# An attention and GLU block on one core: LN2 per tile, GLU in halves, VectorE's exp tiles moved ahead, new scheduler durations

## Chip, core and metric

One core of one Trainium2 chip. The metric is the device time of one execution in microseconds; medians are of several executions. The TensorE clock is given as the granted share of full speed.

## The reference, cut

```python
h  = x + attention(layernorm(x))          # S = 2048, D = 640, 32 heads of 20
h2 = h + (gelu(ln(h) @ w_gate) * (ln(h) @ w_up)) @ w_down   # Df = 1728
```

All tensors are bf16. Terms used below: *QK* is the matmul of queries with keys that makes the scores, *exp* the exponential of the softmax, *PV* the matmul of these exponentials with the values; LN2 is the layernorm before the GLU, whose matmuls are gate, up and down; an *eviction* copies a result out of PSUM. The softmax takes 32 x 2048 x 2048 = 134 million exponentials, and these decide how the kernel is built.

## The kernel before

The kernel describes its work as operations with dependencies and an assumed duration each. While it is built, a list scheduler of its own runs them on paper and fixes each engine's order. Engines then run in that order, each waiting for semaphores.

Attention goes through seven chunks of queries (512, 512, 256, 256, 256, 128, 128). A *tile* is 512 columns of scores of one head. ScalarE gets *units* of three and two tiles in turn, PSUM banks 0 to 2 and 3 to 4; VectorE gets 250 of the 2048 tiles and computes their exponential with integer tricks. Work of the chunk before (output projection `wo`, LN2, GLU) is background of a lower priority.

The heads have 20 channels, so a QK matmul uses 32 of TensorE's 128 rows. Head `j` of a group of four takes row group `j`:

```python
tiles += [(s_, g, kb, j) for g in gs for kb in range(NT // nk) for j in range(4)]
# ...
def qk_mms(out, x, kk):                       # ... cut
    return lambda eng: eng.matmul(out()[:, kk * nq:(kk + 1) * nq],
        kt_all[32 * j:32 * j + 32, g, kt * 128:(kt + 1) * 128],
        qt_all[32 * j:32 * j + 32, q0 // 512, g, q0 % 512:q0 % 512 + nq],
        start=True, stop=True, tile_position=(32 * j, 0), skip_group_check=True)
# ... in unit(u): QK of the unit, then QK of VectorE's tile, if the unit has one
qk = op("pe", fns, 0.215, P_QK, mode="row", ...)
xd = dtile[u]
if xd:
    qd = op("pe", [qk_mms(lambda: bank(bd), xd, kk) for kk in ...], 0.08,
            P_QK + 0.5, mode="row", ..., after=[qk])
```

When TensorE was little used in the last 3.4 us of the scheduler's time, the scheduler puts filler matmuls (`pad`: four small ones side by side; `warm`: one large one) into its free time, and pads beside a PV too. They are meant to keep its clock up.

Of the kernel before, what the change touches and what calls it, by code (L numbers as in the profile page):

```python
# [17 lines left out]
WARM_WIN, WARM_MIN = 3.4, 0.5  # L18
PAD_WIN, PAD_MIN = 3.4, 0.42
PE_AGE = 1.5  # L20

MODE_SWITCH = {"pe": 0.105, "act": 1.28}
# [19 lines left out]
class Sched:  # L42
# [43 lines left out]
    def schedule(self):  # L86
# [22 lines left out]
        while done < total:  # L109
# [4 lines left out]
            for e in ENGINES:  # L114
# [70 lines left out]
                if e == "pe" and self.pad is not None and o.tag and o.tag[0] == "O":  # L185
                    while recent and recent[0][0] < t - PAD_WIN:
                        recent.popleft()
                    u = sum(x for _, x in recent) + o.util
                    while u < PAD_MIN * PAD_WIN and o.util < 1.1:
                        o.fns = o.fns + self.pad  # L190
                        o.dur += 0.215
                        o.util += 0.213
                        u += 0.213
                    live = o.i not in self.final
# [111 lines left out]
PV_QUADS = 2  # L306
D_LAG = 8
PR, PR2 = 12, 6
ND = 4
D_PER_SLOT = (8,) * len(SIZES)  # L310
D_SLOT0 = 2
D_FIRST, D_SPAN = 1, 16
# [5 lines left out]
def bass_sequential_preLN__mha_block__glu_gated_geglu__prompt_kernel(  # L318
# [12 lines left out]
    with ExitStack() as es:  # L331
# [10 lines left out]
        def c_mm(n, passes=1):  # L342
            return 0.001 + passes * n / 2400.0
# [174 lines left out]
        def ln_rsqrt(t0, n, prio, table=False, sqrt=False):  # L518

            y = rs[:, t0:t0 + n]  # L520
            a, b = nw[:, 0, 0:n], nw[:, 1, 0:n]
            ts = range(t0, t0 + n)
            k16, ks = ("mv16", t0), ("sd16", t0)
            rk = [("rs", t) for t in ts]
            v = lambda fn, r, w: op("dve", fn, 0.17, prio, reads=r, writes=w)
            d = v if table or sqrt else lambda fn, r, w: op(POOL, fn, 0.25, prio, reads=r, writes=w)
            d(I("tensor_copy", mv16[:, t0:t0 + n, :], mv[:, t0:t0 + n, :]), [("mv", t) for t in ts], [k16])
            d(I("tensor_scalar", sd16[:, t0:t0 + n], mv16[:, t0:t0 + n, 1], LN_EPS, None, ALU.add), [k16], [ks])
            d(I("tensor_copy", mu[:, t0:t0 + n], mv16[:, t0:t0 + n, 0]), [k16], [("mu", t) for t in ts])
            if sqrt:  # L530
                op("act", I("activation", sd16[:, t0:t0 + n], sd16[:, t0:t0 + n], ACT.Sqrt), 0.2, 1, reads=[ks], writes=[ks])
                v(I("reciprocal", y, sd16[:, t0:t0 + n]), [ks], rk)
                return
            if table:
                op("act", I("activation", sd16[:, t0:t0 + n], sd16[:, t0:t0 + n], ACT.Sqrt), 0.2, -1, mode="sqrt", reads=[ks],
                   writes=[ks])
                v(I("reciprocal", y, sd16[:, t0:t0 + n]), [ks], rk)
                return
            d(I("tensor_copy", a, sd16[:, t0:t0 + n]), [ks], ["nw0"])
            d(I("tensor_scalar", y.bitcast(I32), a.bitcast(I32), -0.5, RSQRT_MAGIC, ALU.mult, ALU.add), ["nw0"], rk)  # L540
            for _ in range(2):
                d(I("tensor_tensor", b, y, y, ALU.mult), rk, ["nw1"])
                d(I("tensor_tensor", b, b, a, ALU.mult), ["nw0", "nw1"], ["nw1"])
                d(I("tensor_scalar", b, b, -0.5, 1.5, ALU.mult, ALU.add), ["nw1"], ["nw1"])
                d(I("tensor_tensor", y, y, b, ALU.mult), ["nw1"] + rk, rk)
            d(I("tensor_tensor", sd16[:, t0:t0 + n], a, y, ALU.mult), ["nw0"] + rk, [ks])
            v(I("reciprocal", y, sd16[:, t0:t0 + n]), [ks], rk)
# [219 lines left out]
        units, ubank, dtile, ends = [], [], [], []  # L767
        i, in_slot = 0, {}
        while i < len(tiles):
# [9 lines left out]
            if k[1] < want and tiles[i][0] == s_:  # L779
                dtile.append(tiles[i])  # L780
                k[1] += 1
                i += 1
            else:
                dtile.append(None)
            k[0] += 1
            ends.append(i)
        assert all(k[1] % 2 == 0 for k in in_slot.values())
        d_tiles = set(x for x in dtile if x)
# [42 lines left out]
        def unit(u):  # L831
# [52 lines left out]
            while pv_wait:  # L884
# [17 lines left out]
                if len(quads) < PV_QUADS and not final:  # L902
                    pv_wait[0:0] = [x for h in quads for x in h]
                    return

                for have in quads:
                    for x in list(d_done):
                        if u - x_unit[x[2]] >= D_LAG and x[2][3] not in [y[2][3] for y in have]:
                            have.append(x)
                            d_done.remove(x)  # L910
                while final and d_done:
                    have = []
                    for x in list(d_done):
                        if x[2][3] not in [y[2][3] for y in have]:
# [20 lines left out]
                if final:  # L935
                    sc.final.add(pv)
                    assert not d_done and not d_raw
# [3 lines left out]
        def base(c):  # L941
            n = CHUNKS[c][1]
            if n == 128:
                return 2 + (c == len(CHUNKS) - 1)
            return 2 * (c % 2) if n < 512 else 0

        def epilogue(s_, bk):
# [13 lines left out]
            for tt in range(4):  # L961
                op("pe", lambda eng, tt=tt: eng.transpose(bank(b2)[:, tt * 128:(tt + 1) * 128],
                                                          osb[:, s, tt * 128:(tt + 1) * 128], identf[:]),
                   c_mm(128, 4), P_EPI, mode="full", reads=[("osb", s), "identf"], writes=[key], acq=[b2] if tt == 0 else [],
# [21 lines left out]
        def post(c, banks, tail):  # L986
# [27 lines left out]
            ln_rsqrt(q0 // 128, nt, p, table=tail)  # L1014
            if tail:
                op("act", I("activation", nm[:, 1:2], off0[:, 0:1], ACT.Gelu_apprx_tanh), 0.2, -1, mode="gelu",
                   reads=["off0"], writes=["warmge"], after=(sc.lw[("sd16", q0 // 128)],))
            for tt in range(tb, tb + nt):
                t = q0 // 128 + tt - tb
                ln_apply("dve", h_sb[:, tt, :], xn_t[:, t % 2, :], ("xn", t % 2), t, [("h", tt, 0), ("h", tt, 1)], p)  # L1020
# [7 lines left out]
            hk = [("hnT", tt) for tt in range(tb, tb + nt)]  # L1028
            hdone = []
            fn_ = 512 // nq  # L1030
            nb = -(-NF // fn_)

            def mms(k, w, wkey, after):
                bk, key = Bank(*banks), ("bk", sc_id())
                for fi in range(min(fn_, NF - k * fn_)):
                    f = k * fn_ + fi
                    for a in range(NA):
                        st = fi == 0 and a == 0
                        op("pe", lambda eng, a=a, f=f, fi=fi: eng.matmul(  # L1039
                            bank(bk)[:, fi * nq:(fi + 1) * nq], w[:, a, F0[f]:F0[f] + 128], hnT[:, a, 128 * tb:128 * tb + nq],  # L1040
                            start=(a == 0), stop=(a == NA - 1)),
                           c_mm(nq), p, mode="full", util=nq / 2400.0, reads=hk + [wkey], writes=[key], acq=[bk] if st else [],
                           after=after if st else ())
                return bk, key

            def cols(k):
                return min(512, (NF - k * fn_) * nq)

            def hv(k, w):
                return ha_f[:, hb + 512 * k:hb + 512 * k + w]  # L1050

            def hkeys(k):
                return [("ha", u) for u in range((hb + 512 * k) // 256, (hb + 512 * k + cols(k)) // 256)]

            if tail:
                for k in range(nb):
                    i = k % 2
                    bg, kg = mms(k, wg, "wg", hdone[k - 2:k - 1] if k >= 2 else ())
                    w = cols(k)
                    s16, fv = zb[:, i, 0:w], hv(k, w)  # L1060
                    op("act", lambda eng, bg=bg, s16=s16, w=w: eng.activation(s16, bank(bg, w), ACT.Gelu_apprx_tanh),
                       c_act(w), -1, mode="gelu", reads=[kg], writes=[("zb", i)], rel=[bg])
                    bu, ku = mms(k, wu, "wu", ())
                    hdone.append(op("dve", lambda eng, bu=bu, s16=s16, fv=fv, w=w: eng.tensor_tensor(  # L1064
                        fv, s16, bank(bu, w), ALU.mult), c_dve(w), p, reads=[ku, ("zb", i)], writes=hkeys(k),
                        rel=[bu]))
            else:

                cp, gl = [], []
                for k in range(nb):  # L1070
                    bg, kg = mms(k, wg, "wg", tuple(x for key in hkeys(k) for x in sc.rd.get(key, ())))
                    w = cols(k)
                    fv = hv(k, w)
                    cp.append(op("dve", lambda eng, bg=bg, fv=fv, w=w: eng.tensor_copy(fv, bank(bg, w)), c_dve(w), p,  # L1074
                                 reads=[kg], writes=hkeys(k), rel=[bg], after=first))
                for ks in [list(range(i, min(i + 4, nb))) for i in range(0, nb, 4)]:
                    w = 512 * (ks[-1] - ks[0]) + cols(ks[-1])
                    fv = hv(ks[0], w)
                    gl.append(op("act", I("activation", fv, fv, ACT.Gelu_apprx_tanh), c_act(w) + 0.04, -1, mode="gelu",
                                 reads=sum(map(hkeys, ks), []), writes=sum(map(hkeys, ks), []), after=cp))  # L1080
                for k in range(nb):
                    w = cols(k)
                    fv = hv(k, w)
                    bu, ku = mms(k, wu, "wu", (sc.lw[hkeys(k)[-1]],))
                    hdone.append(op("dve", lambda eng, bu=bu, fv=fv, w=w: eng.tensor_tensor(fv, fv, bank(bu, w),  # L1085
                                                                                                 ALU.mult),
                                    c_dve(w), p, reads=[ku] + hkeys(k), writes=hkeys(k), rel=[bu]))
            for tt in range(tb, tb + nt):
                t = q0 // 128 + tt - tb
                i = t % 2  # L1090
                for hf in range(2):
                    bk = Bank(*banks)
                    key = ("bk", sc_id())
                    for f in range(NF):
                        o = hb + f * nq + (tt - tb) * 128
                        op("pe", lambda eng, f=f, o=o, hf=hf, bk=bk: eng.matmul(  # L1096
                            bank(bk, 320), ha_f[:, o:o + 128], wd[:, f, hf * 320:(hf + 1) * 320],
                            start=(f == 0), stop=(f == NF - 1)), c_mm(320), p, mode="full", util=0.133, reads=hkeys(f // fn_) + ["wd", "wdz"],
                           writes=[key], acq=[bk] if f == 0 else [], after=hdone[-2:] if f == 0 else ())
# [88 lines left out]
```

## Time and profile before

| | before |
|---|---|
| median, runs | 927.22 us, 3 runs (926.86 to 927.35) |
| head, to the first exp | 35.67 us |
| middle, first exp to end of last | 853.73 us, ScalarE busy 850.12 |
| tail, after the last exp | 36.10 us, TensorE busy 30.74 |
| QK matmuls, busy | 303.4 us |

The cut in three is the key to this kernel: in the middle only what ScalarE waits for counts, in the tail only TensorE. The prediction shows the lines for it. Two more are the recorded lengths of ScalarE's exps by size (count, then busy us and mean ns of one):

```profile
L339 ACT ACTIVATE pts<-ps 128x1536 bf16<-128x1536 f32 x240 | 381.5, 1589 | 4.4 <-PE ps L852 3.7 <-PE ps L339 0.6
L339 ACT ACTIVATE pts<-ps 128x1024 bf16<-128x1024 f32 x240 | 280.5, 1169 | 0.5 <-PE ps L339 0.4
```

A three-tile and a two-tile exp together follow each other every 2.26 us in the chain of the middle, yet their recorded means add up to 1.589 + 1.169 = 2.76 us. So the records of neighbours overlap.

### The profile page before, as it was taken

To read this page: it belongs to the slowest core of one execution; us is meant where nothing else is said; L and a number is where in the kernel's file an instruction comes from. 1 tells how busy PE (TensorE), PEld (TensorE's weight loads), DVE (VectorE), ACT (ScalarE), POOL (GpSimd) and SP (SyncE) were. 2 spreads that over 40 slices of the span, in tenths; PEclk is the share of its full clock that TensorE was granted. 3 is DMA by queue.
4 is the path that set the end of the run, shared out by engine and by line. 5 is a ranking of instruction groups with operands and counts; after the bars stand their busy time and mean duration, and the time that the engine had idled before them with its cause. 6 is when DMAs were issued, how large, how long until landed. Compare 5 with 4: busy or idle time off the path is not lost.

```text
span 925.5 us, 23154 instructions
## 1 busy us (share of the span) xinstructions
PE 845.3 (91%) x10109; PEld 354.8 (38%) x10109; DVE 810.3 (88%) x1703; ACT 885.7 (96%) x801; POOL 35.1 (4%) x117
## 2 busy tenths in 40 slices
PE   3998999999998998999888999999989999999998
PEld 2432322222232222233233333344444445555667
DVE  8859999999898998888798997989998997998873
ACT  6899999999999999999999999999999999999962
POOL 5000000000001000000001000001000000000100
DMA  7301010322550000001021000010100000110000
GB/s 256 95 18 44 18 55 18 90 60 66 152 180 16 15 1 1 1 15 44 1 31 23 9 2 1 16 30 10 37 16 16 9 23 2 31 32 10 10 17 16
DMA packets 39517, 34.36 MB, mean 37 GB/s; under 512 B 19436, under 2 KB 36936, under 8 KB 39416
## 3 DMA queue, kind: packets, MB, share of 16 engines
q1 hardware_dynamic: 39416, 32.89, 12.7%
q8 instruction: 79, 1.29, 0.6%
q14 instruction: 22, 0.18, 0.1%
HBM read 20.12 MB, written 8.09 MB: 30 GB/s over the span
## 4 chain that ended last, share of the span: by engine, by line
ACT 72%; PE 14%; DVE 11%; issue 1%; POOL 0%; DMA 0%
ACT pts L339 46%; ACT rege L339 25%; PE ps L1039 4%; DVE qt_all L339 3%; PE ps L616 3%; PE ps L852 3%; PE ps L339 3%; DVE rege L339 2%; PE ps L1096 2%; DVE qt_all L812 1%; DVE rege L812 1%; DVE stats L339 1%; ACT L339 1%; DVE rege L1074 1%; PE ps L561 0%
## 5 line engine op out<-in xcount | busy, mean ns | idle before, releaser
L339 ACT ACTIVATE pts<-ps 128x1536 bf16<-128x1536 f32 x480 | 573.1, 1379 | 4.9 <-PE ps L852 3.7
L852 PE MATMUL ps<-qt_all,kt_all 32*128 32x256 bf16 (+2 forms) x3584 | 303.4, 289 | 43.2 <-ACT pts L339 27.5
L339 ACT ACTIVATE rege<-ps 128x1536 bf16<-128x1536 f32 x239 | 300.1, 1381 | 2.1 <-PE ps L339 1.5
L852 PEld LDWEIGHTS ps<-qt_all,kt_all 32*128 32x128 bf16 x3584 | 95.0, 92 | 276.8 <-ACT pts L339 160.8
L339 DVE TENSOR_TENSOR qt_all<-qt_all 128x1024 bf16<-128x1024 bf16 (+1 forms) x240 | 164.0, 683 | 3.4
L1039 PE MATMUL ps<-rege,regw 128*128 128x256 bf16 (+2 forms) x980 | 154.7, 290 | 9.9 <-ACT rege L339 4.2
L339 PE MATMUL ps<-pts,v_all 128*21 128x256 bf16 (+2 forms) x2098 | 138.8, 290 | 0.5 <-DVE rege L339 0.5
L812 DVE TENSOR_SCALAR rege<-ps 128x512 int16<-128x512 f32 x154 | 105.3, 685 | 27.6 <-PE ps L852 26.8
L339 DVE TENSOR_SCALAR qt_all<-qt_all 128x1024 bf16<-128x1024 int16 (+1 forms) x288 | 115.8, 417 | 2.5
L339 PE MATMUL ps<-rege,v_all 128*21 128x256 bf16 (+2 forms) x1294 | 113.3, 292 | 0.1
L1039 PEld LDWEIGHTS ps<-rege,regw 128*128 128x128 bf16 x980 | 72.5, 98 | 67.9 <-issue 28.5
L616 PE MATMUL ps<-regw 128*128 128x512 bf16 (+1 forms) x360 | 86.9, 351 | 1.9 <-DVE v_all L749 0.7
L1096 PE MATMUL ps<-regw,rege 128*128 128x320 bf16 x448 | 79.4, 301 | 1.1 <-DVE rege L1064 0.5
L812 DVE TENSOR_SCALAR qt_all<-ps 128x512 int16<-128x512 f32 x96 | 65.6, 684 | 3.7 <-PE ps L852 2.6
L339 DVE TENSOR_SCALAR rege<-rege 128x1024 int16<-128x1024 int16 (+2 forms) x166 | 67.1, 421 | 1.3
L339 DVE TENSOR_TENSOR rege<-rege 128x1024 bf16<-128x1024 bf16 (+3 forms) x103 | 65.5, 644 | 0.9
L339 PEld LDWEIGHTS ps<-pts,v_all 128*21 128x21 bf16 x2098 | 50.2, 91 | 37.2 <-issue 31.6
L339 PE MATMUL ps<-kt_all,zer 128*32 128x512 bf16 x676 | 56.6, 384 | 0.0
L1096 PEld LDWEIGHTS ps<-regw,rege 128*128 128x128 bf16 x448 | 36.7, 97 | 32.4 <-issue 15.8
L339 PEld LDWEIGHTS ps<-rege,v_all 128*21 128x21 bf16 x1294 | 41.0, 91 | 20.6 <-issue 14.3
L1085 DVE TENSOR_TENSOR rege<-rege,ps 128x512 bf16<-128x512 bf16 (+1 forms) x53 | 35.7, 676 | 12.1 <-PE ps L1039 11.8
L616 PEld LDWEIGHTS ps<-regw 128*128 128x128 bf16 x360 | 28.6, 98 | 45.2 <-issue 21.0
(95 smaller groups left out, 574.3 us busy)
## 6 DMA issues: line engine op xcount, KB each, us to landing
rege<-in_A_x_dram SPq DMA_DIRECT2D x6, 640.0 KB, 5.1
q_rows<-regw SPq DMA_DIRECT2D x20, 128.0 KB, 1.7
out_dram<-rege SPq DMA_DIRECT2D x16, 160.0 KB, 2.1
regw<-in_B_w_gate_dram SPq DMA_DIRECT2D x1, 2160.0 KB, 11.9
regw<-in_B_w_up_dram SPq DMA_DIRECT2D x1, 2160.0 KB, 16.9
regw<-in_B_w_down_dram SPq DMA_DIRECT2D x1, 2080.0 KB, 22.9
kt_all<-k_rows SPq DMA_DIRECT2D x12, 160.0 KB
qt_all<-q_rows SPq DMA_DIRECT2D x12, 160.0 KB
```

The lines of the kernel that those rows point to most:

```text
L339: return lambda eng: getattr(eng, method)(*args, **kwargs)
L616: yield op("pe", lambda eng, l=l, r=r, k=k: eng.matmul(bank(bk, n), l, r, start=(k == 0), stop=(k == len(steps) - 1)), c_mm(n), prio, mode ...
L812: d_ops.append(op("dve", lambda eng: eng.tensor_scalar(v[:, 512 * h:512 * h + 512], bank(b), EXP_MUL, -32000.0, ALU.mult, ALU.max), c_dve( ...
L852: return lambda eng: eng.matmul(out()[:, kk * nq:(kk + 1) * nq], kt_all[32 * j:32 * j + 32, g, kt * 128:(kt + 1) * 128], qt_all[32 * j:32 ...
L1039: op("pe", lambda eng, a=a, f=f, fi=fi: eng.matmul(bank(bk)[:, fi * nq:(fi + 1) * nq], w[:, a, F0[f]:F0[f] + 128], hnT[:, a, 128 * tb:128 ...
L1074: cp.append(op("dve", lambda eng, bg=bg, fv=fv, w=w: eng.tensor_copy(fv, bank(bg, w)), c_dve(w), p, reads=[kg], writes=hkeys(k), rel=[bg], ...
L1085: hdone.append(op("dve", lambda eng, bu=bu, fv=fv, w=w: eng.tensor_tensor(fv, fv, bank(bu, w), ALU.mult), c_dve(w), p, reads=[ku] + hkeys( ...
L1096: op("pe", lambda eng, f=f, o=o, hf=hf, bk=bk: eng.matmul(bank(bk, 320), ha_f[:, o:o + 128], wd[:, f, hf * 320:(hf + 1) * 320], start=(f = ...
```

## The change

Intent: LN2 and gate work of a chunk can start after one or two tiles of 128 queries, not after four; the exp tiles on VectorE are computed four (first chunk) to six units earlier and used nine or more units later, so TensorE need not stand at a PV for them; and the scheduler's durations come nearer to measured ones, with a little more filler. The core of the diff:

```diff
-WARM_WIN, WARM_MIN = 3.4, 0.5
-PAD_WIN, PAD_MIN = 3.4, 0.42
-PE_AGE = 1.5
-MODE_SWITCH = {"pe": 0.105, "act": 1.28}
+WARM_WIN, WARM_MIN = 3.4, 0.55
+PAD_WIN, PAD_MIN, PAD_END = 3.4, 0.42, 0.46      # PAD_END: last PV of a slot
+PE_AGE = 1.0
+MODE_SWITCH = {"pe": .098, "act": 1.28}
-D_LAG = 8
+D_LAG = 9
-D_FIRST, D_SPAN = 1, 16
+D_FIRST, D_SPAN, D_LEAD, D_LEAD0, D_HOLD = 1, 16, 6, 4, 4
-            return 0.001 + passes * n / 2400.0
+            return 0.004 + passes * n / 2400.0
+        dtile = [None] * len(units)
+        u = 0
+        for n, x in dplan:                           # n: its unit before
+            u = max(n - (D_LEAD if slots[x[0]][0] else D_LEAD0), u, D_FIRST, ...)
+            dtile[u] = x
+            u += 1
-                   c_mm(128, 4), P_EPI, mode="full", ...      # fp32 transposes
+                   c_mm(128, 2.5), P_EPI, mode="full", ...
-            ln_rsqrt(q0 // 128, nt, p, table=tail)
             for tt in range(tb, tb + nt):
+                ln_rsqrt(t, 1, p, table=tail)
-            fn_ = 512 // nq
+            ns = min(nq, 256)
+            fn_ = 512 // ns                           # gate, GELU, up over sub-chunks of ns
```

Cut: GpSimd scratch per tile, the keys of the halves, the place of a chunk in its buffers, and the selection of VectorE tiles for a PV by slot and age.

## The prediction

> **What bounds the kernel now.** I read the page first, then the busy time of each engine in three stretches, then ScalarE's waits in the middle stretch, then the chain that ended last, and last the timeline of the tail.
>
> ```profile
> span 925.5 us, 23154 instructions
> ...
> PE 845.3 (91%) x10109; PEld 354.8 (38%) x10109; DVE 810.3 (88%) x1703; ACT 885.7 (96%) x801; POOL 35.1 (4%) x117
> ...
> ACT  6899999999999999999999999999999999999962
> ```
>
> ScalarE (ACT) is busy 96% of the span, and its row of slices shows where the other 4% lies: at the two ends. TensorE at 91% and VectorE at 88% are close behind, so either could become the bound if work is added to it. The timeline puts ScalarE's first exp at 35.67 us and the end of its last at 889.40 us. Those two points cut the span into head, middle and tail (columns: PE, its weight loads, DVE, ACT, POOL, granted clock, DMA share, GB/s):
>
> ```profile
> 0.00:35.67 35.67, 21.14 (x154) 12.28 (x154) 30.25 (x97) 24.58 (x45) 12.12 (x32) 1.00 0.55 186
> 35.67:889.40 853.73, 793.37 (x9530) 316.93 (x9530) 765.76 (x1573) 850.12 (x743) 23.00 (x85) 1.00 0.12 32
> 889.40:925.50 36.10, 30.74 (x428) 25.56 (x426) 14.34 (x35) 11.02 (x14) 0.00 (x0) 1.00 0.04 15
> ```
>
> In the middle ScalarE is busy 850.12 of 853.73 us: it idles 3.61 us in all. TensorE idles 853.73 - 793.37 = 60.4 us there and VectorE 88.0 us; that idle time costs nothing as long as ScalarE is fed. In the tail it is TensorE that is busy, 30.74 of 36.10 us, and ScalarE has only 11.02 us of work. ScalarE's waits in the middle (who waited for whom: us in total, times, longest us):
>
> ```profile
> ACT pts L339 <- PE ps L852: 3.7, 1, 3.7
> ACT rege L339 <- PE ps L339: 1.5, 1, 1.5
> ACT pts L339 <- PE ps L339: 0.9, 2, 0.6
> ACT rege L339 <- PE ps L852: 0.7, 2, 0.4
> ```
>
> The first is the wait that ends with the very first exp, so it belongs to the head. What is left is 1.5 + 0.9 + 0.7 = 3.1 us in five waits (the rest of the 3.6 us are crumbs): that is all that feeding ScalarE better can win. The chain that ended last, from the last exp on (start, length, what):
>
> ```profile
> 887.64 3.37 PE ps L1096 x24
> 891.01 0.22 PE ps L1039 x4
> 891.23 1.00 PE ps L339 x48
> 892.23 1.01 PE ps L1039 x16
> ...
> 896.66 1.37 PE ps L616 x10
> ...
> 900.51 1.90 PE ps L339 x8
> 902.41 2.79 PE ps L1039 x50
> 905.21 0.28 PE ps L561 x5
> 905.49 1.90 PE ps L1039 x34
> 907.38 3.80 PE ps L1096 x28
> 911.19 7.05 PE ps L1039 x126
> ```
>
> L1039 is gate and up, L1096 the down projection, L339 x48 the last PV, L616 here the wo projection, L561 a transpose. The x24 are left over from the chunk before the previous one, and of the 280 L1039 in the tail 140 belong to the previous chunk (128 queries: 70 gate, 70 up) and 140 to the last. So the tail is long because TensorE still has background work of earlier chunks when the exps end.
>
> **What the Trainium skill says.** "Trace Analysis", section Identifying Performance Opportunities, says to improve the most contended engine, to take occupancy for it except on TensorE, and that a kernel can have several regimes. The table of three stretches agrees: ScalarE at 99.6% in the middle, TensorE in the tail. "ScalarE: Activation LUTs", section What ACT_TABLE_LOAD costs, gives about 1283 ns for a table load; the trace has 16 loads of mean 1283 ns. "TensorE: Matmul & The Clock Gate", section Back-to-back issue gap, gives N/2.4 + 2.5 ns per warm matmul as the isolated gap and longer figures for small N in a stream with weight loads. Here 126 matmuls of N=128 took 7.05 us, 56.0 ns each, which is the isolated formula. The same page, section What's actually happening, says that the clock is halved after an idle window of about 3.4 us; the trace's granted clock is 1.00 in all three stretches, so more filler matmuls have nothing to win in this kernel as it stands.
>
> **The change part by part**, counted in the two built instruction streams.
>
> *ScalarE* gets the same instructions, one by one: 719 exps, 15 GELU passes, 16 table loads. So the 850 us of the middle stay. This alone bounds the gain: even with no idle time in the middle and unchanged ends, 925.5 - 3.6 = 921.9.
>
> *GLU in halves of 256*: 280 matmuls with N=512 become 560 with N=256. In the trace 20 of N=256 took 2.36 us, less some 0.3 us until the first ends, so 0.109 us each, against 0.2133 us of array time for one of N=512: 280 x (2 x 0.109 - 0.216) = about 0.6 us on TensorE, beside ScalarE in the middle. PSUM evictions and GELU passes keep their number and size.
>
> *LN2 per tile*: GpSimd's chain of 14 small instructions goes from 6 chains to 15. One chain takes 862.72 - 858.49 = 4.2 us, so 9 x 4.2 = 38 us more on an engine that is 4% busy; VectorE gets 9 more reciprocals of 0.16 us, 1.4 us. The last chunk has one tile, so its tail chain is the same. For chunks of 512 queries the first tile's LN can end earlier and the fourth perhaps later (four chains in a row, 17 us); the halves let gate work start after two tiles.
>
> *VectorE exp tiles earlier, PV later*: same number (the 250 evictions of an exp tile stay), other order. It should take away the places where TensorE, in order, stands at a PV for VectorE's tile, such as the 1.5 us wait of the list. I credit 0.7 us of the 3.1.
>
> *Scheduler durations and thresholds*: 372 more small filler matmuls, in groups of four side by side; 12 took 0.82 us, so with a first one of 0.39 us a group adds 0.215 us: 93 x 0.215 = 20.0 us more on TensorE. Ten more warm-up matmuls add 2.2 us. TensorE's idle time in the middle falls from 60 us to some 33 us, counting the 4.3 us that moves in from the tail. That is no cost by itself.
>
> *The tail*: the order of instructions tells most. After the last QK, TensorE has 24 down matmuls and 280 gate/up before, and 0 and 262 after, and 3 warm-up matmuls instead of 8. That is 24 x 0.136 + 18 x 0.056 = 3.3 + 1.0 = 4.3 us of real work less. Through the dependencies, with E the end of the last exp and the durations of the timeline of before:
> - PV: before at E+1.8, behind the 24 down matmuls. After, 26 gate matmuls (1.5 us) lie between the last QK and PV, and fit beside the last exp: PV at E+0.05.
> - wo starts at E+7.1 before; after, PV ends at E+1.05 and the steps from there to wo took 4.3 us (892.2 to 896.5), with one more eviction of 0.6 us in the way but less gate work: about E+5.5.
> - The GELU of the previous chunk starts at E+11.1 before, as the last gate evictions came after wo. After, all gate work is done earlier and GELU starts with its table, E+5.4 + 1.3 = E+6.7, and ends at E+8.4.
> - 68 up matmuls follow, 3.8 us: E+12.3. LN2's square root has its table at E+9.7 and its result on VectorE behind two up evictions at E+12.0: beside the matmuls. Five transposes, 2 more matmuls and the last eviction: E+13.2.
> - 28 down: 3.8 us, E+17.0; 140 gate/up x 0.056 = 7.84 us, E+24.85; eviction 0.5; 28 down and eviction 4.5: E+29.85; store to the end 2.26 us (923.24 to 925.5): E+32.1.
>
> Before it is E+36.1: 4.0 us less, close to the 4.3 us of work moved away.
>
> *Head*: ScalarE's order is the same, TensorE only swaps a few transposes against projections: 0.
>
> Sum: -4.0 (tail) - 0.7 (middle) + 0 (head) = -4.7 us; 927.2 - 4.7 = 922.5. As the new numbers look like ones swept on a chip, I go a little lower: **922.0 us**.
>
> **Rivals.**
> *The middle gets stalls*: 20 us of filler in front of PV on an in-order TensorE, which already waits often for ScalarE before QK, can make a QK late; and PV or gate work can stand for LN2's longer GpSimd series and for DMA transposes. For it: TensorE would be above 96% busy in the middle. Against: most of its waits there are for ScalarE to free a bank, which is slack. It would make +2 to +6 us, 924 to 928.
> *The middle loses its idle time as well*: -3.1 instead of -0.7, so 919.5. For it: the 1.5 us wait is of the kind addressed.
> *The tail is bound by the chain GELU table, GELU, square-root table, LN2*: then moving matmuls away wins only the early part, -2 us, so 924.5. Against: in my steps that chain ends at E+12.0, and TensorE at E+12.3; it is near.
> *The clock falls or rises*: 1.00 throughout, nothing to win; more filler speaks against a loss.
>
> **Range and chances.** Tail -2 to -5, middle -3.1 to +3, head +-0.5, run spread 0.5 us: 918.5 to 926.5 us. A gain over 2% needs 908.7 us, below what ScalarE's unchanged middle allows with any tail here: it would need 14 us more from head and tail. A loss over 2% needs 18 us of new stalls.
>
> **What would show it.** Right: ScalarE's busy time within 1 us of 885.7; last exp ending between 886 and 889; the tail 32 us with GELU soon after its table load, no down matmuls ahead of the last PV; TensorE busy near 865 us. Wrong: a list of new ScalarE waits on PV or QK in the middle summing to more than 3 us, the tail still near 36 us, or a granted clock other than 1.00.

## More of the kernel before

The four batches of experiments ran on different chips (runs 1 to 4, 5 to 8, 9 to 11, 12); the kernel before ran in each, with medians of 927.39, 927.88, 927.73 and 927.64 us, so ratios are taken within a batch.

The tile for VectorE is the one that follows the unit's tiles in the list, so its `j` is another one:

```python
units.append(tiles[i:i + len(bs)])
i += len(units[-1])
if k[1] < want and tiles[i][0] == s_:
    dtile.append(tiles[i]); i += 1
else:
    dtile.append(None)
```

## The result

The changed kernel took 928.46 us (928.03 to 928.96, 4 runs) against 927.09 us (4 runs) for the kernel before: ratio 1.0015, 95% interval 0.9998 to 1.0032. Ratios here are the mean time of one kernel's fast runs over that of the other's fast runs of the same rounds, so not quite the ratio of the medians quoted. The time is the same, and outside the range of 918.5 to 926.5 us.

The same three stretches show where the two effects cancel. First exp at 35.37 us, last exp's end at 893.80 us; the columns are those of the prediction's table:

```profile
35.37:893.80 858.43, 831.65 (x10218) 365.62 (x10250) 769.17 (x1586) 854.60 (x743) 56.09 (x211) 1.00 0.12 32
893.80:926.00 32.20, 25.83 (x375) 21.52 (x375) 12.86 (x31) 11.02 (x14) 0.00 (x0) 1.00 0.03 12
```

The head is 0.3 us shorter and the tail 36.10 - 32.20 = 3.9 us, nearly as worked out. The middle is 858.43 - 853.73 = 4.7 us *longer*, where 0.7 us less was expected. ScalarE's waits in it, the counterpart of the list in the prediction:

```profile
ACT pts L340 <- PE ps L860: 4.5, 5, 3.7
ACT pts L340 <- PE ps L340: 1.1, 1, 1.1
```

Without the head's 3.7 us they sum to 1.9 us, less than before. Instead ScalarE's *busy* time, which counts overlapping records once (their *union*), rose from 850.12 to 854.60 us, with the same 743 instructions of the same sizes. The prediction had held these 850 us for fixed. The groups by size tell why:

```profile
L340 ACT ACTIVATE pts<-ps 128x1536 bf16<-128x1536 f32 x240 | 362.8, 1512 | 6.5 <-PE ps L860 4.5 <-PE ps L340 1.1
L340 ACT ACTIVATE pts<-ps 128x1024 bf16<-128x1024 f32 x240 | 262.1, 1092 | 0.0
```

On average an exp is recorded *shorter* than before (1512 against 1589 ns, 1092 against 1169), and still the union of all is longer. The records of neighbours overlap less. In the trace after, a three-tile exp that comes late is recorded with 1.45 us, and each one on time after it with about 0.03 us more than the last, until the next late one. An instruction that comes late starts later behind its neighbour, and most of the lost time shows neither as a listed wait nor as a longer instruction.

So I took the ends of all 719 exps from both traces. In both, a three-tile exp ends 1.343 us after the exp before it when it is on time. Call one late when it is over that by more than 0.01 us (for two-tile exps, over 0.917), leaving out the five behind a GELU with its table loads. Before, 16 are late, by 4.6 us in all; after, 81, by 9.4 us. The difference, 4.8 us, is the longer middle. After, all 81 are three-tile exps, most of them 0.02 to 0.3 us late. For those the time from the end of the exp that frees their banks to the end of the shorter two-tile exp beside it is all the slack there is.

What holds TensorE up? Its busy rows for QK, in the page of before and of after:

```profile
L852 PE MATMUL ps<-qt_all,kt_all 32*128 32x256 bf16 (+2 forms) x3584 | 303.4, 289 | 43.2 <-ACT pts L339 27.5
```

```profile
L860 PE MATMUL ps<-qt_all,kt_all 32*128 32x256 bf16 (+2 forms) x3584 | 329.7, 288 | 16.2 <-ACT pts L340 6.2
```

The same 3584 matmuls keep TensorE busy 26.3 us longer, and its idle time before QK, in which it mostly waits for ScalarE to free a bank (good waiting), fell from 43.2 to 16.2 us. Nothing in the change alters a QK matmul. But it alters its neighbour: moved six units ahead, VectorE's tile no longer stands beside tiles that use the three other row groups. Counting from the plan, none of the 250 tiles shares a row group with its unit before; 173 do after (331 matmuls, as a tile of a chunk under 512 queries takes two or four). I call these *collisions*.

### The profile page after: what moved, and what is told of

Same layout as the page of the kernel before. It is cut to its first block, busy times and chain, and to the rows that moved or that the text cites. A ratio compares the mean times of both kernels' runs of the same rounds, so it can differ in the third digit from the quotient of the medians.

```text
span 926.0 us, 24582 instructions
## 1 busy us (share of the span) xinstructions
PE 878.1 (95%) x10739; PEld 399.4 (43%) x10771; DVE 812.3 (88%) x1712; ACT 890.2 (96%) x801; POOL 68.2 (7%) x243
## 3 DMA queue, kind: packets, MB, share of 16 engines
q1 hardware_dynamic: 39416, 32.89, 12.6%
## 4 chain that ended last, share of the span: by engine, by line
ACT 47%; PE 45%; DVE 4%; DMA 1%; POOL 1%; issue 1%; SPq 0%
ACT pts L340 30%; ACT rege L340 16%; PE ps L860 14%; PE ps L1056 10%; PE ps L340 10%; PE ps L1117 6%; PE ps L619 4%; DMA regw<-in_A_wqkv_dram 1%; DVE qt_all L340 1%; PE ps L978 1%; ACT L340 1%; DVE qt_all L820 1%; PE ps L564 1%; POOL nw L340 1%; DVE rege L1105 0%
## 5 line engine op out<-in xcount | busy, mean ns | idle before, releaser
L340 ACT ACTIVATE pts<-ps 128x1536 bf16<-128x1536 f32 x480 | 564.3, 1302 | 6.5 <-PE ps L860 4.5
L860 PE MATMUL ps<-qt_all,kt_all 32*128 32x256 bf16 (+2 forms) x3584 | 329.7, 288 | 16.2 <-ACT pts L340 6.2
L340 ACT ACTIVATE rege<-ps 128x1536 bf16<-128x1536 f32 x239 | 290.2, 1299 | 0.8
L860 PEld LDWEIGHTS ps<-qt_all,kt_all 32*128 32x128 bf16 x3584 | 109.6, 92 | 226.9 <-ACT pts L340 96.2
L1056 PE MATMUL ps<-rege,regw 128*128 128x256 bf16 (+1 forms) x1260 | 159.2, 262 | 6.7 <-ACT rege L340 4.7
L340 PE MATMUL ps<-pts,v_all 128*21 128x256 bf16 (+2 forms) x2098 | 142.3, 290 | 1.1 <-DVE osb L340 0.9
L1056 PEld LDWEIGHTS ps<-rege,regw 128*128 128x128 bf16 x1260 | 98.9, 98 | 60.9 <-issue 35.2
L340 PE MATMUL ps<-kt_all,zer 128*32 128x512 bf16 x1048 | 85.8, 384 | 0.0
L619 PE MATMUL ps<-regw 128*128 128x512 bf16 (+1 forms) x342 | 80.7, 348 | 2.2 <-issue 0.8
## 6 DMA issues: line engine op xcount, KB each, us to landing
regw<-in_B_w_up_dram SPq DMA_DIRECT2D x1, 2160.0 KB, 13.2
```

The source lines that it names most:

```text
L340: return lambda eng: getattr(eng, method)(*args, **kwargs)
L619: yield op("pe", lambda eng, l=l, r=r, k=k: eng.matmul(bank(bk, n), l, r, start=(k == 0), stop=(k == len(steps) - 1)), c_mm(n), prio, mode ...
L1056: op("pe", lambda eng, a=a, f=f, fi=fi: eng.matmul(bank(bk)[:, fi * ns:(fi + 1) * ns], w[:, a, F0[f]:F0[f] + 128], hnT[:, a, 128 * b:128 * ...
```

## The experiments

Theory A: the collisions are the loss. Rival B: the 372 additional small fillers and the tighter durations are. Rival C came up later: the lead itself has another effect.

The table gives each run's median, its ratio to the kernel before in the same rounds, and from its profiled run the length of the middle and the tail, QK's busy time, and the late exps (number, sum; in brackets what single delays of 1.2 us or more add to it).

| run | us | ratio | middle | tail | QK busy | late |
|---|---|---|---|---|---|---|
| before | 927.22 | | 853.73 | 36.1 | 303.4 | 16, 4.6 us (1.6) |
| after | 928.46 | 1.0015 | 858.43 | 32.2 | 329.7 | 81, 9.4 us (1.2) |
| 1 free row groups, same order | 922.57 | 0.9943 | 852.97 | 32.1 | 308.6 | 23, 3.7 us (1.2) |
| 2 before with collisions, same order | 930.45 | 1.0027 | 856.34 | 36.3 | 330.1 | 39, 7.2 us (1.6) |
| 3 row-group rule | 922.86 | 0.9947 | 854.91 | 30.3 | 311.1 | 38, 5.7 us |
| 4 after, less filler | 929.39 | 1.0019 | 856.81 | 34.2 | 329.3 | 59, 7.7 us |
| 5 after, no lead | 934.41 | 1.0071 | 863.25 | 32.8 | 308.2 | 31, 14.1 us (8.4) |
| 6 rule, LN2 and GLU as before | 925.15 | 0.9973 | 854.94 | 32.3 | 309.1 | 33, 5.8 us |
| 7 rule, old durations | 924.29 | 0.9967 | 855.83 | 30.7 | 309.5 | 16, 6.7 us (3.2) |
| 8 rule, look ahead | 925.92 | 0.9982 | 861.90 | 29.6 | 318.3 | 46, 12.7 us (5.9) |
| 9 before, lead with rule alone | 929.10 | 1.0034 | 859.71 | 30.8 | 311.2 | 21, 10.5 us (3.2) |
| 10 rule, less filler | 922.63 | 0.9945 | 854.78 | 30.2 | 311.5 | 29, 5.6 us (2.6) |
| 11 before, more filler | 934.53 | 1.0072 | 859.85 | 37.2 | 305.1 | 15, 10.7 us (5.7) |
| 12 rule, more filler only early | 922.25 | 0.9945 | 852.62 | 31.8 | 311.2 | 27, 3.5 us |

Runs 1 and 2 give wrong results (relative error 0.73 and 0.67): some scores are computed with another head's data. All others are correct. Where this text calls one faster or slower, the 95% interval of its ratio excludes 1.

The middle minus the sum of the last column lies between 849.0 and 849.3 us in all fourteen profiles. So late exps account for the whole difference of the middles, and the question is only what makes them late. (The expectations quote an earlier count, 83 late three-tile exps after and 43 by 6.3 us in run 3, which took in exps right behind table loads.)

### 1. The changed kernel with free row groups

```diff
+js = [y[3] for y in tl]
+xq = xd if xd[3] not in js else xd[:3] + (min(j for j in range(4) if j not in js),)
-qd = op("pe", [qk_mms(lambda: bank(bd), xd, kk) ...
+qd = op("pe", [qk_mms(lambda: bank(bd), xq, kk) ...
```

I compared the built programs: every engine has the same instructions in the same order with the same waits.

> The changed kernel, instruction for instruction in the same order with the same waits; only the 173 of the 250 VectorE score tiles whose QK stands beside a QK of the same row group of TensorE (same head j of four) now use a free row group (the wrong head's data: the result is wrong on purpose). Theory A (moving the tiles ahead broke the packing of four row groups: each such QK waits for its neighbour, about 0.2 us of TensorE each): the TensorE busy time of the QK line falls from 330 us back to about 305, most of the 83 late three-bank exps are on time again, the middle shortens by 3 to 6 us, time 923 to 925.5. Rival B (the 372 more filler matmuls and the tighter durations make the QKs late): QK busy may fall but the time stays within 1 us of 928.4.

All came as theory A says, the time even a little below its range: 922.57 us, ratio 0.9943, interval 0.9926 to 0.9959. The stretch of the middle and the QK row of its page, with all fillers and durations of the change kept:

```profile
36.08:889.05 852.97, 821.12 (x10255) 353.46 (x10258) 766.26 (x1586) 850.76 (x743) 57.57 (x211) 1.00 0.12 32
L860 PE MATMUL ps<-qt_all,kt_all 32*128 32x256 bf16 (+2 forms) x3584 | 308.6, 289 | 22.8 <-ACT pts L340 11.5
```

The middle is 5.5 us shorter than after and 0.8 us shorter than before, which is what was predicted for the change. The same two instructions in both timelines show the single collision (start, length; x4 are a unit's three tiles and VectorE's one):

```profile
304.55 0.60 PE L860 MATMUL ps<-qt_all,kt_all 32*128 32x512 bf16 x4
...
313.64 0.61 PE L860 MATMUL ps<-qt_all,kt_all 32*128 32x512 bf16 x4
```

That was the changed kernel; here is this run, with the row groups free:

```profile
304.25 0.40 PE L860 MATMUL ps<-qt_all,kt_all 32*128 32x512 bf16 x4 [0.18 <-ACT pts L340]
...
313.30 0.40 PE L860 MATMUL ps<-qt_all,kt_all 32*128 32x512 bf16 x4
```

Four tiles on four row groups take 0.40 us together; when two share a group, 0.60. And in the first pair the sign of the wait turns: with free groups TensorE waits 0.18 us for ScalarE, with the collision it is TensorE that comes late. An estimate from this, with the price of N=512 taken for all 173 tiles: 173 x 0.20 = 35 us of TensorE work. The QK row shows 329.7 - 308.6 = 21 us of it; that row counts the union of overlapping records.

### 2. The kernel before with collisions

The same edit on the kernel before, with `xq = xd[:3] + (js[0],) if u % 10 < 7 else xd`: 180 of 250 collide. Order and waits are unchanged.

> The kernel before in the same order with the same waits, but 180 of its 250 VectorE score tiles use the row group of the first tile of the unit beside them (wrong result on purpose). Theory A: QK busy rises from 303 to about 330 us and the middle lengthens by 2 to 6 us, time 929 to 933, with no filler added. Rival B: the kernel before has room on TensorE, the time stays within 1 us of 927.1.

930.45 us, ratio 1.0027 (interval 1.0012 to 1.0042). QK busy 330.1 us as expected, the middle 2.6 us longer, the tail unchanged. So collisions alone cost time with not one filler or duration touched. They cost less here than the 5.5 us of middle that run 1 won back. TensorE's idle time in the middle may explain that: 60.4 us before and 44.0 in this run, against 26.8 in the changed kernel; I have no run that varies it alone.

### 3. A rule instead of wrong data

```diff
+            while x[3] in [y[3] for y in units[u]]:
+                u += 1
+            assert u <= n
             dtile[u] = x
```

> The changed kernel with one more rule: a VectorE tile moved ahead goes to the first unit from its place on that holds no tile of the same row group; right results, new order. Theory A: no collisions, tail still near 32 us, middle near 853 us, so 921 to 924. Rival B: 927 to 929.

922.86 us (922.66 to 922.98), ratio 0.9947, interval 0.9932 to 0.9962, right results: faster than both kernels. The middle stays 1.2 us longer than before, with 38 late exps; the order is a new one, with 940 small fillers instead of 1048. The tail is 1.8 us shorter than after.

### 4. The changed kernel with the old filler thresholds

```diff
-WARM_WIN, WARM_MIN = 3.4, 0.55
-PAD_WIN, PAD_MIN, PAD_END = 3.4, 0.42, 0.46
+WARM_WIN, WARM_MIN = 3.4, 0.5
+PAD_WIN, PAD_MIN, PAD_END = 3.4, 0.42, 0.42
```

> The changed kernel with the two filler thresholds as before (0.5 and no 0.46): 836 small filler matmuls instead of 1048, collisions kept. Theory A: TensorE gains 11 us of idle time but QK busy stays near 330; a part of the late exps goes, 926 to 928. Rival B: the middle goes back near 853 us and the time to 924 or less.

Against rival B: with 212 fillers less the time is 929.39 us. The middle wins 1.6 us, the tail loses 2.0, and 59 exps are still late by 7.7 us. The expectation of A (926 to 928) missed too, by the tail, which it did not consider.

### 5. The changed kernel without the lead

```diff
-D_LAG = 9
+D_LAG = 8
-... D_LEAD, D_LEAD0, D_HOLD = 1, 16, 6, 4, 4
+... D_LEAD, D_LEAD0, D_HOLD = 1, 16, 0, 0, 4
```

> The changed kernel with the VectorE tiles back in their old units and the old PV lag (lead 0, lag 8); everything else of the change kept. No collisions, as in the kernel before. Theory A alone (the collisions are the whole loss and the lead itself is worth nothing): QK busy near 304 us, middle near 853 us, tail by its instruction order (about 1 us more TensorE work left than in the changed kernel) 33 us, so 923 to 924. Rival C (the lead and the later PV do keep TensorE from standing at a PV for VectorE's tile, so without them the middle has other waits): middle 855 us or more, 925 to 930.

934.41 us, slower than all runs so far and outside both forecasts. Theory A *alone* fails: one wait of ScalarE makes most of the difference. The two longest rows of ScalarE's waits up to 890 us (sum, count, longest, us):

```profile
ACT pts L340 <- PE ps L860: 12.6, 5, 8.3
ACT pts L340 <- PE ps L340: 0.9, 1, 0.9
```

The 8.3 us lie before 149.41 us, where ScalarE's exps turn to a new group of heads. (The 12.6 also hold the 3.7 us before the first exp.) The timeline has the softmax bounds of that group stored to memory from 142.38 us and read back from 144.27, after an eviction on VectorE at 141.68; the first QK follows at 148.97, behind nine projection matmuls that ended only then. The kernel before waits 1.6 us near there and the changed one does not. So the lead has a worth of its own, or reorders this place luckily. This run can't tell these apart, as an order changes as a whole. Without that one delay (8.4 us by the ends of the exps) the middle would be 854.8 us, between A's 853 and C's 855. The tail is 32.8 us, close to the 33 us expected without the lead.

### 6. Row-group rule, LN2 and GLU as before

`post` (LN2, GLU and what follows) is taken from the kernel before; the rest, the split GpSimd scratch too, stays as in run 3.

> The run with the row-group rule (922.9 us), with LN2 per chunk and GLU over the whole chunk as in the kernel before. If LN2 per tile and the halves are what shortens the tail, the tail goes from 30.4 back to about 35 us and the time to 926 to 928; if they are worth little (the tail is decided by where the scheduler puts the rest of the background work, and by the count of instructions it stays near 32 us), 922 to 925.

925.15 us: the middle is the same to 0.1 us and the tail 1.9 us longer (32.3). LN2 per tile and the halves are worth some 2 us, all in the tail. They are not the larger part of the tail's gain.

### 7. Row-group rule, old TensorE durations

```diff
# lines joined
-PE_AGE = 1.0         MODE_SWITCH "pe": .098    c_mm 0.004    c_mm(128, 2.5)
+PE_AGE = 1.5         MODE_SWITCH "pe": 0.105   c_mm 0.001    c_mm(128, 4)
```

> The run with the row-group rule (922.9 us), with the scheduler's old TensorE durations (matmul constant, four passes for the fp32 transpose, mode switch, age). If the tighter durations take away slack that QK needs, the middle gets shorter than 854.9 us by 1 to 3 us and the number of late exps (43) falls; the tail by instruction order 32 us; 921 to 924. If they help, the middle gets longer.

Late exps fall from 38 to 16, as they should if the old durations held hidden slack, and the middle still is 0.9 us longer: a single delay of 3.2 us at 143 us, the same turn as in run 5, outweighs it.

### 8. Row-group rule with a look ahead

```diff
# condensed
+if p[0] > 0 and t - o.ready < 6.0 and t + o.dur + switch > tq + 0.2:   # tq: next QK can start
+    skipped.append((p, i)); continue
```

The same bound limits fillers.

> The run with the row-group rule, plus a look ahead in the scheduler: no other TensorE work or filler may start if by the scheduler's own durations it would end more than 0.2 us after the next QK can start. If the 43 late exps left (6.3 us) come from work put too close before a QK, half of them go: 919 to 921.5, with a tail of 30 us or less by instruction order. If not, 922 to 924.

It failed. Three of four runs had a clock below 1.00 (0.993 and twice 0.996); the profiled run has 46 late exps, among them four delays of 1.3 to 1.6 us around 646 to 654 us and at 822 us. Its clock record has half speed for 10.2 us from about the same time and for 3.4 us later on. That holding work back left TensorE too idle is the likely reason; no run shows it. The one run at 1.00 took 924.0 us.

### 9. The kernel before with the lead and the rule alone

Built from run 3 with LN2, GLU, durations and fillers as before.

> The kernel before with one part of the change alone, VectorE tiles ahead with the later PV, plus the row-group rule (LN2, GLU, durations and filler as before). By its instruction order the tail holds 22.3 us of TensorE work against 26.6 before: tail 31 to 32.5 us. If the lead also takes away the waits of ScalarE at the group changes (0.7 and 1.6 us before, 8.4 and 3.2 us in the last two runs without the lead or with the old durations), middle 852 to 855 us: 921 to 924. If the lead needs LN2 per tile and the halves, tail above 34 us and 925 or more.

The tail comes out at 30.8 us, so the lead with the rule brings a short tail without the rest. The middle does not hold: 3.2 us at 143 us again and seven smaller delays from 0.4 to 1.1 us. All four runs had a clock of 0.989 to 0.998, with 712 fillers in this order. 929.1 us.

### 10. Row-group rule with the old filler thresholds

> The run with the row-group rule (922.9 us), with the filler thresholds as before: 720 small filler matmuls instead of 940. If filler in front of QK makes a part of the 43 late exps, the middle gets 1 to 2 us shorter and the time is 920.5 to 922.5 with a tail near 30 us. If filler guards the clock, one or more of the four runs show a clock below 1.00 and 2 us more.

922.63 us, ratio 0.9945. Fewer fillers come with fewer late exps here, 29 in place of 38. But the clock is at half speed for one window of 3.4 us, from 70.4 us, in the record of the profiled run, and two exps there are 1.3 us late each, so that the sum stays at 5.6 us; all four runs show 0.998.

### 11. The kernel before with more filler

`WARM_MIN` 0.55 alone: 924 small fillers instead of 676.

> The kernel before with the higher warm-up threshold alone (0.55): 924 small filler matmuls instead of 676, no collisions. Theory A: filler alone does not make QKs late, QK busy stays near 303 us, late exps about 20 to 35, the tail by its order 36.5 us, so 926 to 929. Rival B: the late exps rise to 60 or more and the time over 930.

934.53 us, ratio 1.0072 (interval 1.0057 to 1.0087). Rival B's time (over 930) comes and A's does not; B's mechanism, 60 or more late exps, does not come either: there are 15. The loss is in seven single delays of 0.7 to 2.7 us, five of them before 280 us; the clock is 1.00. ScalarE's waits in the middle:

```profile
ACT pts L339 <- PE ps L339: 5.2, 6, 1.5
ACT pts L339 <- PE ps L852: 3.0, 3, 2.5
ACT rege L339 <- PE ps L339: 0.9, 1, 0.9
```

So more filler, put into this order, can cost as much as the collisions do, in another way. Neither theory has a name for these delays; see below what stays open.

### 12. Row-group rule, more filler for the first 100 us only

The thresholds of the change hold while the scheduler's time is under 100 us, those of before after it.

> The run with the row-group rule and the old filler thresholds (922.6 us, one clock dip of 3.4 us near 71 us in the span that makes two exps late by 2.6 us), with the changed kernel's thresholds kept for the first 100 us of the schedule and the old ones after. If the dip is what that run lost, the clock stays 1.00, no exp is over 1 us late, the middle is 852 to 853.5 us and the time 919.5 to 921.5 us, the fastest of all; if not, 922 to 924.

922.25 us (5 runs, 921.72 to 923.21), ratio 0.9945, interval 0.9931 to 0.9958. The dip at 70 us is gone and the middle is 852.62 us, as expected; the time is not (919.5 to 921.5), as all five runs show a dip, in the profiled run from 893.9 us, in the tail, which is 31.8 us instead of 30.2. Runs 3, 10 and 12 can't be told apart by time, and all three beat both kernels by 0.5 to 0.7%.

## Why the prediction was wrong

- **Bound, and cut in three: right.** The time of each run follows from its middle, its tail and a head of 34.9 to 36.4 us.
- **Tail: right.** 32.1 us worked out, 32.20 measured, and by steps with E the end of the last exp: GELU at E+6.7 against 900.27 - 893.80 = 6.5, the first of the two down projections at E+13.2 against 13.1, the 140 gate/up at E+17.0 against 17.1, the last down at E+25.35 against 25.4. These lines of the chain that ended last answer to those shown in the prediction:

```profile
893.82 1.00 PE ps L340 x55
...
900.27 1.71 ACT rege L340
...
902.02 3.97 PE ps L1056 x68
...
906.90 3.98 PE ps L1117 x28
910.88 7.83 PE ps L1056 x140
...
919.21 3.99 PE ps L1117 x28
```

- **Head: right**, 0.3 us.
- **Middle: wrong, and here the prediction fell.** The step is "*VectorE exp tiles earlier, PV later*: same number ..., other order", with 0.7 us credited. It counted instructions and did not ask what stands beside each. In its place: the QK of 173 tiles land on a busy row group (0.20 us more in the case shown), TensorE's idle time in the middle falls to 26.8 us (predicted: 33), its busy time in all is 878.1 us (predicted: near 865), and 81 exps come late by 9.4 us. Run 1 takes only this away and gives 922.57 us and a middle of 852.97; the prediction had 922.0 and 853.0. Run 2 puts only this into the kernel before and makes it slower.
- **The 0.7 us: partly luck.** In run 1 the 1.5 us wait that the prediction named is gone and the listed waits sum to 1.5 us instead of 3.1; but the lateness outside the listed waits rose from 1.5 to 2.2 us. The two together make the 0.8 us. Nor were the 3.1 us of waits "all that feeding ScalarE better can win": late exps cost the kernel before 4.6 us.
- **The rival "the middle gets stalls" named the sign and size (+2 to +6), but for other causes**, filler, GpSimd's chains and DMA transposes. Run 1 keeps all of these as they are in the changed kernel and still has a middle of 852.97 us. Its own sign, TensorE over 96% busy in the middle, did come (831.65 of 858.43 us, 96.9%). The sign listed at the end, "a list of new ScalarE waits ... summing to more than 3 us", did not: the loss sat in busy time.
- **"More filler matmuls have nothing to win": too strong.** The kernel before, whose profiled run shows 1.00, had a clock of 0.998 in one run in each of the first three batches of experiments, at 929.6 to 929.8 us instead of about 927.7. The changed kernel's four runs and those of run 3 had none. But a dip need not cost that much: runs 10 and 12 had one in every execution and are no slower than run 3.
- **GLU's halves, filler and reciprocals as work**: beside ScalarE, as predicted. Fillers' busy time rose from 56.6 to 85.8 us for 372 matmuls, counted as a union of records; 20 us was predicted as work.

**What stays open.** The tail is short with the lead and the rule alone (run 9, 30.8 us) and also with the rest of the change without the lead (run 5, 32.8 us), against 36.1 us before. So the parts do not add up, and why the scheduler leaves less work for the end in each case was not followed. And the single delays of 1 to 8 us in the first 300 us, when K, Q and the bounds are still being made, come and go with changes of order (runs 5, 7, 9, 11): run 5's was followed to a late first QK of a group of heads, the others were not tracked down.

## What to carry to other kernels

When a matmul uses part of the array, its cost depends on the neighbour it is issued with: before moving one, list what shares its row group, and teach the scheduler that duration. When an engine is near 100% busy, don't read its waits alone: compare its busy time for the same instructions and the spacing of their ends, as lateness can hide there. And when a gain doesn't appear, cut the span where the bound changes: a part may have come as predicted and another cancelled it.

## What the Trainium skill lacked or had wrong

- "TensorE: Matmul & The Clock Gate", section The mechanism (of Part 3), says that weight loads overlap running matmuls only when their row groups differ, and shows four tiles on four groups. The trace agrees, and it gives a price that the page lacks: four tiles of N=512 take 0.40 us on four groups and 0.60 us when two share one.
- The same page, section Back-to-back issue gap, gives about 81 ns per matmul for N=128 in a stream with weight loads. Here 140 took 7.83 us, 55.9 ns each, weight loads included, which is the page's isolated formula N/2.4 + 2.5.
- "Trace Analysis", section Identifying Performance Opportunities, takes occupancy of ScalarE as a fair measure of how close it is to its limit. Here ScalarE was 99.6% busy in the middle before and after, with the same instructions showing 850.12 and 854.60 us of busy time, and the mean record of a three-tile exp fell from 1589 to 1512 ns as the middle got 4.7 us longer. No page says that a late instruction shows as less overlap of records.
